# Zero fills copied inside HBM, and one more V window kept on the chip, in a single-token attention layer with its gradients

## The chip, the cores and the metric

The kernel runs on one core of one Trainium2 chip. The metric is the device time of one execution in microseconds (us). Before the change three runs took 816.24, 816.43 and 816.74 us: a median of 816.43 us.

## What is computed

One token passes through a pre-norm attention layer with a cached sliding window and through a bilinear feed-forward layer; the kernel computes the output and the gradients of all inputs for a given output gradient. Cut to what matters:

```
W = 4096                                   # of Sk = 32768 cached positions
k, v = k_cache[:, :, Sk-W:], v_cache[:, :, Sk-W:]        # 8 groups, 256 wide
h  = x + softmax(q k^T / 16) v @ wo,       q = layernorm(x) @ wq
h2 = h + ((n @ w_gate) * (n @ w_up)) @ w_down,   n = layernorm(h)
outputs: h2, and the gradients of x, k_cache, v_cache, wq, wo, w_gate, w_up, w_down
```

The gradients of the two caches (out_2 for K, out_3 for V) are as large as the caches: 8 groups of 32768 x 256 bf16, 16 MB a group. Only the last 4096 positions of a group, 2 MB, carry a gradient. The other 28672 positions, 14336 KB a group, are zero and must be written as zeros: 16 such regions, 234.88 MB together.

## The kernel before

**Two streams.** The zero regions ("fills") are issued by SyncE (`FILL`, hardware queue q1 of the profile), all loads and all other stores by GpSimd (`IO`, software queue q0). Both queues run on the same 16 DMA engines. Each engine's issue order is program order, so a wait of one GpSimd instruction holds all its later DMAs.

**Fills.** Line 58 sets a tile `zeros` of 128 partitions x 8192 bf16 (16 KB a partition) to zero on VectorE. Lines 59 to 62 issue, for each group, a fill of out_2 and one of out_3, whose source is that tile, read 7 times (`NZ`) through a broadcast dimension. 16 fills, each of 896 rows of 16 KB.

**Forward part, by groups g = 0 to 7 (from line 344).** A K or V window is 2 MB, 16 KB a partition, and lies in one of 8 slots of the tile `S`. `K_SLOT` and `V_SLOT` (lines 35, 36) say which: V of groups 0 to 4 have slots 0 to 4 to themselves, K goes around slots 5, 6 and 7, V of 5 and of 6 both use slot 6, and V of 7 takes slot 5. `load_K` and `load_V` call `load_window` (line 79). `scores` transposes K on TensorE and multiplies it with q; `softmax` makes the weights; `moments` (lines 309 to 335) scales K by the weights on VectorE (line 318) and contracts it with V on TensorE (lines 322, 325, 329). V of 5, 6 and 7 share places with other windows, so their loads wait until those are used up: V of 6 waits for the moments of group 5, V of 7 for those of group 6. The halves `woA` and `woB` of the attention's output weight are then loaded over slots 6 and 5 (lines 361 and 376), and the feed-forward weights over slot 7 and the tile `Rt` (lines 377, 378).

**Middle.** Output projection (line 383), feed-forward layer, its gradient and the gradient at the attention output (lines 383 to 460).

**Backward part, by groups (from line 562).** V is transposed again (line 568), the two gradients of a window are made as outer products (line 602), evicted into two of four staging slots 5, 6, 7 and 0 (`STG`) and stored (line 607). V of groups 5, 6 and 7 is no longer on the chip: `V_AGAIN` (line 37) loads it again into slots 1, 2 and 3, once those groups' own V has been used. Gradients of the weights are made in between (`side`, stored at line 477).

Of the kernel before, what the change touches and what calls it, by code (L numbers as in the profile page):

```python
# [7 lines left out]
bf16 = mybir.dt.bfloat16  # L8
# [5 lines left out]
D = 448  # L14
NI = 7
H = 16
G = 8
Dh = 256
W = 4096
T = 32  # L20
F = 1792
FC = 14
Sk = 32768
EPS = 1e-5
SCALE = 1.0 / 16.0
SLOT = T * Dh
NS = 8
NV = 5
HQ = H * Dh // 2
HF = F // 2  # L30
ZW = 8192
NZ = (Sk - W) * Dh // (128 * ZW)


K_SLOT = [5, 6, 7, 5, 6, 7, 5, 7]
V_SLOT = [0, 1, 2, 3, 4, 6, 6, 5]
V_AGAIN = {5: 1, 6: 2, 7: 3}


@with_exitstack  # L40
def kernel(
# [3 lines left out]
    V_, S_, P_ = nc.vector, nc.scalar, nc.tensor  # L45
    FILL = nc.sync
    IO = nc.gpsimd

    const = ctx.enter_context(tc.tile_pool(name="const", bufs=1))
# [4 lines left out]
    FILL.dma_start(out=x_bf[:], in_=A_x.rearrange("a b d -> (a b) d"))  # L54
    go_bf = const.tile([1, D], bf16, tag="rowb", name="go_bf")
    FILL.dma_start(out=go_bf[:], in_=grad_out.rearrange("a b d -> (a b) d"))
    zeros = const.tile([128, ZW], bf16)
    V_.memset(zeros[:], 0.0)
    for g in range(G):
        for o in (out_2, out_3):  # L60
            reg = o[0, g, 0:Sk - W, :].rearrange("s d -> (s d)").rearrange("(p n f) -> p n f", p=128, f=ZW)
            FILL.dma_start(out=reg, in_=zeros[:].unsqueeze(1).to_broadcast([128, NZ, ZW]))


    S = const.tile([128, NS, SLOT], bf16)
    Mt = const.tile([128, G, 2, 2 * Dh], f32)
    Rt = const.tile([128, SLOT], bf16)

    def slot(k):
        return S[:, k, :]  # L70

    def slot_kv(k):
        return S[:, k, :].rearrange("p (t d) -> p t d", d=Dh)

    Kw = [slot_kv(k) for k in K_SLOT]
    Vw = [slot_kv(k) for k in V_SLOT]

    def load_window(dst, cache, g):
        IO.dma_start(out=dst, in_=cache[0, g, Sk - W:, :].rearrange("(p t) d -> p t d", t=T))  # L79

    def load_K(g):
        load_window(Kw[g], A_k_cache, g)

    def load_V(g):
        load_window(Vw[g], A_v_cache, g)
# [174 lines left out]
    def products(Xw, vecT, g, out_ps):  # L260

        for q in range(8):
            tr = ps.tile([128, 4, 2, 128], bf16, tag="tr", bufs=2)
            for i in range(4):
                for dh in range(2):
                    P_.transpose(tr[:, i, dh, :], Xw[:, 4 * q + i, dh * 128:(dh + 1) * 128], ident_bf[:])  # L266
            xt = kt_buf()
            evac(xt, tr[:])
            for i in range(4):
                for dh in range(2):  # L270
                    P_.matmul(out_ps[:, 4 * q + i, :], lhsT=xt[:, i, dh, :], rhs=vecT[:, 4 * g + dh:4 * g + dh + 3:2],
                              start=(dh == 0), stop=(dh == 1))
# [6 lines left out]
    def scores(g):  # L279
        sT[g] = fps.tile([128, T, 2], f32, tag="sT", bufs=2, name="sT")  # L280
        products(Kw[g], qT, g, sT[g])

    def softmax(g):
        s = sT[g]
        pmax = small.tile([128, 2], f32, tag="pmax")
        V_.reduce_max(out=pmax[:], in_=s[:].rearrange("p t h -> p h t"), axis=AX)
        mt = ps.tile([2, 128], f32, tag="tmp", bufs=1)
        P_.transpose(mt[:], pmax[:], ident_f[:])
        gmax = small.tile([2, 1], f32, tag="gmax")
        V_.reduce_max(out=gmax[:], in_=mt[:], axis=AX)  # L290
        gd = small.tile([2, 2], f32, tag="gd")
        V_.tensor_scalar(out=gd[:], in0=ident_f[0:2, 0:2], scalar1=gmax[:, 0:1], scalar2=-SCALE, op0=ALU.mult, op1=ALU.mult)
        nb = ps.tile([128, 2], f32, tag="tmp", bufs=1)
        P_.matmul(nb[:], lhsT=ones_f[0:2, :], rhs=gd[:], start=True, stop=True)
        nbias = small.tile([128, 2], f32, tag="nbias")
        V_.tensor_copy(out=nbias[:], in_=nb[:])
        e = small.tile([128, T, 2], f32, tag="e_f")
        sums = small.tile([128, 2], f32, tag="psums")
        for h in range(2):
            S_.activation(out=e[:, :, h], in_=s[:, :, h], func=ACT.Exp, bias=nbias[:, h:h + 1], scale=SCALE, accum_out=sums[:, h:h + 1])  # L300
        rs = small.tile([128, 2], f32, tag="rsum")
        V_.reciprocal(out=rs[:], in_=total(sums[:], 2)[:])
        pf = small.tile([128, T, 2], f32, tag="p_f")
        V_.tensor_tensor(out=pf[:], in0=e[:], in1=rs[:].unsqueeze(1).to_broadcast([128, T, 2]), op=ALU.mult)
        V_.tensor_copy(out=pT_all[:, g], in_=pf[:])
        p_f[g] = pf

    def moments(g):

        K, Vv, pf = Kw[g], Vw[g], p_f[g]  # L310
        MT = fps.tile([128, 2, 2 * Dh], f32, tag="MT", name="MT")
        acc = fps.tile([128, 8], f32, tag="acc", name="acc")
        for c in range(T // 2):
            pk = pk_buf()
            for i in range(2):
                t = 2 * c + i
                for h in range(2):
                    V_.tensor_scalar(out=pk[:, i, h, :], in0=K[:, t, :], scalar1=pf[:, t, h:h + 1], scalar2=None, op0=ALU.mult)  # L318
            for i in range(2):
                t = 2 * c + i  # L320
                for hf in range(2):
                    P_.matmul(MT[:, hf, :], lhsT=Vv[:, t, hf * 128:(hf + 1) * 128], rhs=pk[:, i, :, :].rearrange("p h d -> p (h d)"),  # L322
                              start=(t == 0), stop=(t == T - 1))
                for hf in range(2):
                    P_.matmul(acc[:, 2 * hf:2 * hf + 2], lhsT=Vv[:, t, hf * 128:(hf + 1) * 128], rhs=pT_all[:, g, t, :],  # L325
                              start=(t == 0 and hf == 0), stop=(t == T - 1), skip_group_check=True)
                for h in range(2):
                    for dk in range(2):
                        P_.matmul(acc[:, 4 + 2 * h + dk:5 + 2 * h + dk], lhsT=pk[:, i, h, dk * 128:(dk + 1) * 128], rhs=ones_bf[:, 0:1],  # L329
                                  start=False, stop=(t == T - 1), skip_group_check=True)  # L330
        S_.copy(out=Mt[:, g, 0, :], in_=MT[:, 0, :])  # L331
        V_.tensor_copy(out=Mt[:, g, 1, :], in_=MT[:, 1, :])
        V_.tensor_copy(out=oT_f[:, 4 * g:4 * g + 4].rearrange("p (h f) -> p f h", f=2), in_=acc[:, 0:4].rearrange("p (f h) -> p f h", h=2))
        V_.tensor_copy(out=kbar[:, 4 * g:4 * g + 4], in_=acc[:, 4:8])
        V_.tensor_copy(out=oT_bf[:, 4 * g:4 * g + 4], in_=oT_f[:, 4 * g:4 * g + 4])

    wo_v = A_wo.rearrange("(b p) n -> p b n", p=128)
    woA = S[:, 6, 0:16 * D].rearrange("p (b n) -> p b n", n=D)
    woB = S[:, 5, 0:16 * D].rearrange("p (b n) -> p b n", n=D)
    wg_sb = S[:, 7, 0:NI * HF]  # L340
    wu_sb = Rt[:, 0:NI * HF]
    bc2 = [S[:, 7, NI * HF:NI * HF + F].rearrange("p (i c) -> p i c", i=2), Rt[:, NI * HF:NI * HF + F].rearrange("p (i c) -> p i c", i=2)]
# [6 lines left out]
    for g in range(G):  # L349
        if g + 1 < NV:  # L350
            load_V(g + 1)
        if g + 2 < 7:
            load_K(g + 2)
        if g == 5:
            load_V(5)
        if g == 6:
            load_V(6)
            load_K(7)
        if g == 7:
            load_V(7)  # L360
            IO.dma_start(out=woA, in_=wo_v[:, 0:16, :])
        softmax(g)
        if g + 1 < G and g != 6:
            scores(g + 1)
        moments(g)
        if g == 6:
            scores(7)
        if g == 0:

            t = ps.tile([128, D], f32, tag="tmp", bufs=1)  # L370
            P_.matmul(t[:], lhsT=ones_bf[0:1, :], rhs=go_bf[:], start=True, stop=True)
            S_.copy(out=dh2_bc[:], in_=t[:])
            for c in range(FC):
                V_.tensor_tensor_reduce(out=wd0[:, c, :], in0=wd0[:, c, :], in1=dh2_bc[:], scale=1.0, scalar=0.0,
                                        op0=ALU.mult, op1=ALU.add, accum_out=d_hh[:, c:c + 1])
# [184 lines left out]
    for g in range(G):  # L560
        if g in V_AGAIN:
            Vw[g] = slot_kv(V_AGAIN[g])
        dp = bps.tile([128, T, 2], f32, tag="dp")
        for q in range(8):
# [6 lines left out]
            for i in range(4):  # L571
                for dh in range(2):
                    P_.matmul(dp[:, 4 * q + i, :], lhsT=xt[:, i, dh, :], rhs=doT[:, 4 * g + dh:4 * g + dh + 3:2],  # L573
                              start=(dh == 0), stop=(dh == 1))
        for again, sl in V_AGAIN.items():
            if sl == g:
                load_window(slot_kv(sl), A_v_cache, again)
# [19 lines left out]
        for c in range(T // 2):  # L597
            d_ps = bps.tile([128, 2, 2, Dh], f32, tag="d2", bufs=2)
            for i in range(2):
                t = 2 * c + i  # L600
# [39 lines left out]
```

## Time and profile before

| what | value |
|---|---|
| median of three runs | 816.43 us |
| profiled execution, time | 816.48 us |
| profiled execution, span | 814.7 us |
| busy: TensorE / VectorE / ScalarE / GpSimd | 504.1 / 374.4 / 165.0 / 40.4 us |
| fills, queue q1 | 234.88 MB, 68.3% of 16 engines' span |
| loads and stores, queue q0 | 103.00 MB, 30.2% of 16 engines' span |
| HBM read / written | 57.28 / 280.59 MB |

The time is 1.8 us longer than the span of the profiled instructions. The span is cut into 40 slices in which a digit is a busy share in tenths. A DMA queue's share is the time that its packets took, over the time of 16 engines. A packet here is one run of bytes that one engine moves; its queue, size, start and duration are recorded. "To landing" is from a DMA's issue to the moment all 16 engines have finished their parts.

### The profile page before, as it was taken

What the parts mean: (1) busy time and instruction counts of PE and PEld (TensorE: products, weight loads), DVE (VectorE), ACT (ScalarE), POOL (GpSimd) and SP (SyncE); (2) the same over time, 40 slices, a digit from 0 to 9 for tenths busy, and PEclk for the clock granted to TensorE, in tenths of its full rate; (3) what the DMA queues carried; (4) which work ended last, traced back from release to release, by engine and by line L of the source; (5) the groups of instructions that cost most, each with busy time, mean ns of one, the idle gap of its engine ahead of it and who ended that gap; (6) DMA issues with size and microseconds to landing.
All of it is one profiled execution on the core that took longest, in us unless ns stands there. A gap on an engine that the chain in (4) does not pass through costs nothing.

```text
span 814.7 us, 12155 instructions
## 1 busy us (share of the span) xinstructions
PE 504.1 (62%) x4991; PEld 301.7 (37%) x4991; DVE 374.4 (46%) x1149; ACT 165.0 (20%) x261; POOL 40.4 (5%) x75
## 2 busy tenths in 40 slices
PE   3559969999566947062995562597597848263200
PEld 3445646666434524031983421243143313010000
DVE  4128837776451644028733470754553626253200
ACT  0230211221101000001012231243343424142100
POOL 3000000000000001000001000001000010000000
PEclk9959878999785969565556555555555555555555
DMA  8999999999999999999999999999999999999993
GB/s 344 430 423 427 430 428 429 425 428 426 430 417 426 415 424 420 428 429 431 426 427 429 409 415 421 431 423 422 404 430 425 425 413 423 421 425 427 424 427 170
DMA packets 24573, 338.66 MB, mean 416 GB/s; under 512 B 1251, under 2 KB 1317, under 8 KB 4677
## 3 DMA queue, kind: packets, MB, share of 16 engines
q1 hardware_dynamic: 14596, 234.88, 68.3%
q0 software_dynamic: 9920, 103.00, 30.2%
q8 instruction: 39, 0.64, 0.3%
q14 instruction: 18, 0.14, 0.0%
HBM read 57.28 MB, written 280.59 MB: 415 GB/s over the span
## 4 chain that ended last, share of the span: by engine, by line
issue 59%; DMA 17%; PE 11%; DVE 4%; POOL 3%; ACT 1%; POOLq 0%; DVEq 0%
DMA S<-in_A_wo_dram 4%; DMA Rt<-in_A_wq_dram 4%; DMA out_dram<-Mt 3%; PE dq_ps L453 3%; DMA S<-in_A_k_cache_dram 3%; DMA S<-in_A_v_cache_dram 2%; PE MT L322 2%; POOL out_dram L477 1%; POOL S L79 1%; DVE Rt L423 1%; POOL out_dram L607 1%; PE dh_ps L159 1%; PE d_ps L602 1%; PE tr L568 1%; PE t L413 1%
## 5 line engine op out<-in xcount | busy, mean ns | idle before, releaser
L602 PE MATMUL d_ps<-R,Mt 32*128 32x512 bf16 x256 | 124.4, 612 | 94.4 <-DVE S L212 93.6
L322 PE MATMUL MT<-Rt,S 128*128 128x512 bf16 x512 | 156.8, 391 | 21.1 <-DMA S<-in_A_v_cache_dram 19.9
L318 DVE TENSOR_SCALAR Rt<-S,pf 128x256 bf16<-128x256 bf16 x512 | 117.8, 283 | 32.0 <-PE acc L329 17.3
L212 DVE CAST S<-d_ps 128x512 bf16<-128x512 f32 x128 | 86.8, 689 | 57.1 <-ACT S L210 43.9
L210 ACT CAST S<-d_ps 128x512 bf16<-128x512 f32 x128 | 75.1, 587 | 171.6 <-PE d_ps L602 171.6
L266 PE MATMUL tr<-ident_bf,S 128*128 128x128 bf16 x512 | 52.5, 267 | 44.5 <-DMA S<-in_A_k_cache_dram 41.2
L602 PEld LDWEIGHTS <-Mt 32*128 32x128 bf16 x256 | 23.2, 113 | 148.1 <-issue 146.7
L325 PEld LDWEIGHTS <-S 128*128 128x128 bf16 x512 | 49.9, 98 | 62.7 <-issue 6.6
L568 PE MATMUL tr<-ident_bf,S 128*128 128x128 bf16 x512 | 68.8, 304 | 3.5 <-ACT Mt L210 3.5
L329 PE MATMUL acc<-ones_bf,Rt 128*128 128x1 bf16 x1024 | 61.8, 163 | 0.0
L568 PEld LDWEIGHTS <-S 128*128 128x128 bf16 x512 | 48.5, 135 | 28.0 <-issue 27.8
L266 PEld LDWEIGHTS <-S 128*128 128x128 bf16 x512 | 41.4, 121 | 42.9 <-DMA S<-in_A_k_cache_dram 41.7
L210 ACT COPY Rt<-tr 128x1024 bf16<-128x1024 bf16 x32 | 32.4, 1012 | 84.7 <-PE tr L266 84.3
L325 PE MATMUL acc<-pT_all,S 128*128 128x2 bf16 x512 | 49.1, 165 | 0.0
L329 PEld LDWEIGHTS <-Rt 128*128 128x128 bf16 x1024 | 44.5, 96 | 0.0
L212 DVE COPY Rt<-tr 128x1024 bf16<-128x1024 bf16 x32 | 22.1, 690 | 48.5 <-PE tr L266 47.0
L210 ACT COPY Mt<-tr 128x1024 bf16<-128x1024 bf16 x32 | 32.4, 1014 | 56.3 <-PE tr L568 29.2
L322 PEld LDWEIGHTS <-S 128*128 128x128 bf16 x512 | 32.0, 97 | 21.7 <-DMA S<-in_A_v_cache_dram 20.4
L331 ACT COPY Mt<-MT 128x512 f32<-128x512 f32 x8 | 4.7, 586 | 164.8 <-PE MT L322 145.4
L573 PEld LDWEIGHTS <-Mt 128*128 128x128 bf16 x512 | 19.9, 108 | 36.7 <-DVE Mt L212 13.7
L573 PE MATMUL dp<-doT,Mt 128*128 128x2 bf16 x512 | 22.6, 168 | 12.3 <-DVE Mt L212 10.5
L212 DVE COPY Mt<-tr 128x1024 bf16<-128x1024 bf16 x32 | 22.0, 686 | 16.4 <-PE tr L568 11.3
(182 smaller groups left out, 435.1 us busy)
## 6 DMA issues: line engine op xcount, KB each, us to landing
out_dram<-zeros SPq DMA_DIRECT2D x16, 14336.0 KB, 149.7
out_dram<-S POOLq DMA_DIRECT2D x16, 2048.0 KB, 29.5
S<-in_A_v_cache_dram POOLq DMA_DIRECT2D x11, 2048.0 KB, 35.6
S<-in_A_k_cache_dram POOLq DMA_DIRECT2D x8, 2048.0 KB, 28.0
out_dram<-Mt POOLq DMA_DIRECT2D x6, 896.0 KB, 22.3
S<-in_A_wq_dram POOLq DMA_DIRECT2D x1, 3584.0 KB, 14.7
S<-in_A_wo_dram POOLq DMA_DIRECT2D x2, 1792.0 KB, 35.4
out_dram<-Mt POOLq DMA_DIRECT2D x3, 1024.0 KB, 35.7
```

The costliest lines, as they stand in the source:

```text
L79: IO.dma_start(out=dst, in_=cache[0, g, Sk - W:, :].rearrange("(p t) d -> p t d", t=T))
L210: S_.copy(out=out, in_=in_)
L212: V_.tensor_copy(out=out, in_=in_)
L266: P_.transpose(tr[:, i, dh, :], Xw[:, 4 * q + i, dh * 128:(dh + 1) * 128], ident_bf[:])
L318: V_.tensor_scalar(out=pk[:, i, h, :], in0=K[:, t, :], scalar1=pf[:, t, h:h + 1], scalar2=None, op0=ALU.mult)
L322: P_.matmul(MT[:, hf, :], lhsT=Vv[:, t, hf * 128:(hf + 1) * 128], rhs=pk[:, i, :, :].rearrange("p h d -> p (h d)"), start=(t == 0), stop=( ...
L325: P_.matmul(acc[:, 2 * hf:2 * hf + 2], lhsT=Vv[:, t, hf * 128:(hf + 1) * 128], rhs=pT_all[:, g, t, :], start=(t == 0 and hf == 0), stop=(t ...
L329: P_.matmul(acc[:, 4 + 2 * h + dk:5 + 2 * h + dk], lhsT=pk[:, i, h, dk * 128:(dk + 1) * 128], rhs=ones_bf[:, 0:1], start=False, stop=(t == ...
L453: P_.matmul(dq_ps[:, 2 * h + dk:2 * h + dk + 1], lhsT=Mt[:, h // 2, hf, c0:c0 + 128], rhs=doT_f[:, 2 * h + hf:2 * h + hf + 1], start=(hf = ...
L568: P_.transpose(tr[:, i, dh, :], Vw[g][:, 4 * q + i, dh * 128:(dh + 1) * 128], ident_bf[:])
L573: P_.matmul(dp[:, 4 * q + i, :], lhsT=xt[:, i, dh, :], rhs=doT[:, 4 * g + dh:4 * g + dh + 3:2], start=(dh == 0), stop=(dh == 1))
L602: P_.matmul(d_ps[:, i, :, :].rearrange("p w d -> p (w d)"), lhsT=rows[32 * k:32 * k + 32, a, :], rhs=R[32 * k:32 * k + 32, :], start=True, ...
```

## The change

The zero tile becomes slot 8 of `S` (now 9 slots), so it is a place for a window like any other. Only the two fills of group 0 read it. The 14 fills of groups 1 to 7 are copies from HBM to HBM: their source is the first run of each partition row of the region of out_2, group 0, which the first fill has written, so they wait for that fill to land. The source run is 8192 elements, read 7 times; for the two fills of group 3 it is 28672 elements (56 KB), read twice. V of group 5 is loaded into slot 8 once both fills of group 0 have landed, and stays. V of 6 takes slot 6 at the place where V of 5 was loaded; V of 7 also goes to slot 6, after the moments of group 6, in two DMAs of 16 positions a partition each. `woA` moves to slot 5 and is issued right behind the second half of V of 7, `woB` to slot 6. In the backward part two windows are loaded again in place of three, into slots 1 and 2.

```diff
-NS = 8
-NV = 5
+NS = 9
+NV = 6
+LONG = 28672
+LONG_G = (3,)
-V_SLOT = [0, 1, 2, 3, 4, 6, 6, 5]
-V_AGAIN = {5: 1, 6: 2, 7: 3}
+V_SLOT = [0, 1, 2, 3, 4, 8, 6, 6]
+V_AGAIN = {6: 1, 7: 2}
...
-    zeros = const.tile([128, ZW], bf16)
-    V_.memset(zeros[:], 0.0)
-    for g in range(G):
-        for o in (out_2, out_3):
-            reg = o[0, g, 0:Sk - W, :].rearrange("s d -> (s d)").rearrange("(p n f) -> p n f", p=128, f=ZW)
-            FILL.dma_start(out=reg, in_=zeros[:].unsqueeze(1).to_broadcast([128, NZ, ZW]))
+    zeros = S[:, 8, 0:ZW]
+    V_.memset(zeros, 0.0)
+    def region(o, g, f):
+        return o[0, g, 0:Sk - W, :].rearrange("s d -> (s d)").rearrange("(p n f) -> p n f", p=128, f=f)
+    for g in range(G):
+        for o in (out_2, out_3):
+            if g == 0:
+                FILL.dma_start(out=region(o, g, ZW), in_=zeros.unsqueeze(1).to_broadcast([128, NZ, ZW]))
+            else:
+                f = LONG if g in LONG_G else ZW
+                n = NZ * ZW // f
+                FILL.dma_start(out=region(o, g, f), in_=region(out_2, 0, f)[:, 0:1, :].to_broadcast([128, n, f]))
...
+    def load_half(dst, cache, g, t0):
+        t1 = t0 + T // 2
+        return IO.dma_start(out=dst[:, t0:t1, :], in_=cache[0, g, Sk - W:, :].rearrange("(p t) d -> p t d", t=T)[:, t0:t1, :])
...
-    woA = S[:, 6, 0:16 * D].rearrange("p (b n) -> p b n", n=D)
-    woB = S[:, 5, 0:16 * D].rearrange("p (b n) -> p b n", n=D)
+    woA = S[:, 5, 0:16 * D].rearrange("p (b n) -> p b n", n=D)
+    woB = S[:, 6, 0:16 * D].rearrange("p (b n) -> p b n", n=D)
...
         if g == 5:
-            load_V(5)
+            load_V(6)
         if g == 6:
-            load_V(6)
             load_K(7)
-        if g == 7:
-            load_V(7)
-            IO.dma_start(out=woA, in_=wo_v[:, 0:16, :])
...
         moments(g)
         if g == 6:
+            for t0 in (0, T // 2):
+                v7 = load_half(slot_kv(V_SLOT[7]), A_v_cache, 7, t0)
+            with tc.issue_after(v7.ins):
+                IO.dma_start(out=woA, in_=wo_v[:, 0:16, :])
             scores(7)
```

## The prediction

> **What bounds the kernel now.** I read the slices first, then the queues, then the landing of the fills, then the stretches of the end. From the page:
>
> ```profile
> span 814.7 us, 12155 instructions
> ...
> DMA  8999999999999999999999999999999999999993
> GB/s 344 430 423 427 430 428 429 425 428 426 430 417 426 415 424 420 428 429 431 426 427 429 409 415 421 431 423 422 404 430 425 425 413 423 421 425 427 424 427 170
> DMA packets 24573, 338.66 MB, mean 416 GB/s; under 512 B 1251, under 2 KB 1317, under 8 KB 4677
> ...
> q1 hardware_dynamic: 14596, 234.88, 68.3%
> q0 software_dynamic: 9920, 103.00, 30.2%
> ...
> HBM read 57.28 MB, written 280.59 MB: 415 GB/s over the span
> ```
>
> The 16 DMA engines are busy from the first slice to the last but one, at 404 to 431 GB/s, while no compute engine is (PE has 62%). The rate is the same whether GpSimd's queue loads (first half) or stores (second half). So the time is bytes over rate plus the two ends, and a wait on a compute engine costs nothing while a fill stands in q1 to use the engines. The stretches of the end (columns: length, then busy time of PE, PEld, DVE, ACT, POOL, then PEclk, DMA share, GB/s):
>
> ```profile
> 440.00:760.00 320.00, 202.91 (x1315) 89.09 (x1313) 153.93 (x285) 108.69 (x167) 20.17 (x33) 0.50 1.01 421
> 760.00:795.00 35.00, 0.22 (x1) 0.00 (x0) 0.70 (x2) 0.59 (x1) 1.06 (x2) 0.50 1.01 427
> 795.00:814.70 19.70, 0.00 (x0) 0.00 (x0) 0.00 (x0) 0.00 (x0) 0.00 (x0) 0.50 0.38 161
> ```
>
> Compute ends at about 762 us; the DMA engines then work off what is queued. After 795 they run out one by one (share 0.38). In the packet records the last store ends at 798.0, most engines finish the last fill at 797 to 805, and the last one at 813.1. So the busiest engine sets the end, and whatever every engine is spared comes off the time. The fills' landings, from the answer on the zero tile:
>
> ```profile
> L62 SPq DMA_DIRECT2D out_dram<-zeros x16: 597/46418/62679, 5.2 to 641.0; - x16
> ...
> DMA to landing us min/median/max: 63.3/149.7/187.2
> ```
>
> The first fill, issued at 5.2, lands at 68.5; the packet records put the end of the second at 135. Packets: of 16 KB, loads and stores alike have a median of 611 ns (91% of the fills' within 625); of 8 KB, 309 ns; the fixed part is then 2 x 309 - 611 = 7 ns, the rest 16384 B in 604 ns = 27.1 GB/s an engine.
>
> **The change, part by part,** against the profiled execution's 816.48 us (span 814.7; 0.05 above the median of 816.43).
>
> 1. *One V window less.* 2 MB are 128 packets of 16 KB, 8 an engine: 8 x 611 = 4.89 us off every engine. No other load or store goes: -4.89.
>
> 2. *Longer packets.* Two fills of 56 rows an engine become 16 rows of 56 KB an engine: 112 packets become 32, 80 x 7 ns = 0.56: -0.56.
>
> 3. *V of 7 in halves.* 16 packets of 309 ns for 8 of 611: +0.06.
>
> 4. *The source of 14 fills.* An engine moves 14 x 56 = 784 packets' worth (16 KB) of copies. Before has no copy inside HBM, so both ends are open. Above: if reading and writing HBM took turns, a packet would cost 2 x 611 ns and the sum 784 x 0.611 = +479 us. A nearer high row is the 39 instruction packets of q8, 16 KB at a median of 942 ns: 784 x 0.331 = +260 us. Below: a copy leaves SBUF out, and if SBUF were what holds the pace, it would be shorter; but 16 KB take 611 ns out of HBM and into it alike, the slope from 8 to 12 to 16 KB is one (309, 460, 611), and no shorter packet of this size is to be found (lowest 608), so I take this for the engine's own pace and exclude a gain. I take the nearest row, 611 ns: **0**, and keep the high ends. What speaks for it: the stretch 40 to 360 us, with many loads beside the fills, runs at 425 GB/s, as the pure writing at the end does. What speaks against it: HBM now is read by the fills too. Read and written were 57.28 + 280.59 = 337.9 MB; 14 x 14.68 = 205.5 MB are added and 2.1 go: 541 MB in 811 us is 667 GB/s on average, where the trace shows no more than 431.
>
> The Trainium skill speaks against this part: "HBM Reference", Specifications, gives a domain about 716 GB/s, so a copy with the engines to itself would get 358 of the 427 it could move. By that figure the stretches in which q0 is quiet grow, and I estimate from it some 36 us more, about 847 instead of 811; no run so far asks for more than 431.
>
> 5. *The copies' wait.* The first copy waits on SyncE for fill 0 (68.5). Behind it stand only the other 13 copies, and nothing else uses that queue. The second zero-tile fill is on the engines from 66.6 to 135, so they have work: 0. Without that cover the engines would idle for an issue and a landing.
>
> 6. *V of 5 into slot 8.* Its load waits for both fills of group 0, 135, and stands in GpSimd's queue between K loads that were issued at 108.05 and 145.52. All later loads are behind it; 10 us of cover, so 0. Should fill 1 land later than 145.5, every later load is late by the difference.
>
> 7. *Loads of the forward part.* The chain of waits had:
>
> ```profile
> 279.34 17.70 DMA S<-in_A_v_cache_dram
> ...
> 315.17 33.41 DMA S<-in_A_wo_dram
> ```
>
> V of 6 is now there a group earlier (its load takes the old place of V of 5 at 197), V of 7 comes in halves as the moments of 6 release them, woA behind it. The chain may be some 18 us ahead at 317 us. Late next is woB, which still waits for the last moments. It gains nothing at the end, since the engines are full: 0. In the backward part two reloads remain where three were (issued at 473, 533 and 562): in step 1 already.
>
> 8. *The long packets beside loads.* Fills 6 and 7 (group 3; counted from 0) ran from 305 to 389, and wo, w_gate and w_up are issued at 280 to 318. If the two queues take turns packet by packet, a small packet of wo (7 KB, 272 ns) waits for 2.1 us (3.5 x 0.604) in place of 0.6. A half of wo has 16 such packets' worth an engine: 16 x 1.5 = 24 us, for both halves and the two feed-forward weights of 8 packets each up to 72, less the 18 of step 7: the chain late by at most 54. The last store is issued at 762 and q1 works until 800: 38 us are covered, and TensorE is busy only 203 of 320 us from 440 on, which takes up the rest. At cost 0; without the cover 16.
>
> Sum: 816.48 - 4.89 - 0.56 + 0.06 = **811.1 us**.
>
> **The rivals.**
>
> A. *Copies cost what fills cost* (forecast): 811.1. Against it only step 4's HBM sum. Its own range is 808.5 to 813.5, for the end of the busiest engine.
>
> B. *HBM holds the copies back where q0 is quiet* (the other side). Where q0 moves a lot, a copy has half the packets and HBM is asked for less; where q0 has nothing, all 427 GB/s are copies and HBM is asked for 854. In the packet records q0 moves under 60 GB/s in eight stretches of 20 us between 160 and 440 us, and q1 has 93% of the bytes there: 148 us. At the price of the 942 ns row they grow by 0.54: +80, 891 us; at the price of 611 nothing. It decides as soon as copies in these stretches take over 3.6% longer (5.4 of 148 us). For it: twice the demand that any slice shows. Against: the flat rate over every mix of reads and writes. Its middle is 811.1 + 40 = 851.
>
> C. *Every copy is slow*: between 811.1 + 260 = 1071 and 811.1 + 479 = 1290. For it speaks only that no row shows a copy.
>
> D. *The gain is lost on the way*: the chain of step 8 outlasts its cover, or the busiest engine is not relieved; 811.1 + up to 16, most likely within 0.2% of before (814.8 to 818.1; about what a measurement of this kernel can tell from no change).
>
> **How the numbers follow.** A 0.55, B 0.33, C 0.06, D 0.06. The likeliest is A: 811.1. Faster by over 0.2%: A, 0.55; within 0.2%: D, 0.06; slower: B and C, 0.39. The range begins at 808, below A's steps, and must reach into B: up to 870 it holds A, D and almost three quarters of B, 0.55 + 0.06 + 0.23 = 0.84; C and B's upper end (0.16) are left out. A alone would be 808.5 to 813.5.
>
> **What would show it.** Right: packets of q1 of 16 KB still near 611 ns and of 56 KB near 2.12 us; slices of 425 GB/s throughout; 336.6 MB in all; HBM read near 261 MB; fill 0 still landing at 68 and no gap in the DMA row after it; V of 5 issued at 135. B: long q1 packets and slices well under 420 GB/s between 160 and 440 us, normal ones after 480; the first copies then take longer than the 42 to 45 us of fills 2 to 5. C: such slices everywhere from 135 on. D: packets of 611 ns, but slices under 8 near the end, with the last stores issued after 800. What would make the forecast wrong is step 4 alone; all other steps together are under 20 us.

## The result, and the profile after

The change makes the kernel slower: 906.38 us (four runs, 904.2 to 907.5) against 816.39 (four runs of before), a ratio of 1.110 [1.108, 1.112]. The profiled execution took 906.39 us. The page after, the lines that answer to those shown of before:

```profile
span 904.6 us, 12152 instructions
...
DMA  8999999999999999999999999999999999999995
GB/s 351 429 426 428 425 430 415 355 363 369 369 356 349 327 380 364 353 324 314 348 343 367 378 396 383 400 395 377 410 381 382 384 393 399 380 407 404 320 317 189
DMA packets 23293, 336.56 MB, mean 372 GB/s; under 512 B 1251, under 2 KB 1317, under 8 KB 4677
...
q1 hardware_dynamic: 13316, 234.88, 70.1%
q0 software_dynamic: 9920, 100.90, 28.6%
...
HBM read 260.70 MB, written 280.59 MB: 598 GB/s over the span
```

The DMA engines are as busy as before and move 2.1 MB less, yet need 90 us more: "busy" now means packets that take longer. The GB/s row tells where. Its first six slices (22.6 us each) are those of before; from the seventh on, where the first copy starts, it lies between 314 and 415 until the tail, and never comes back. HBM read is 203 MB higher. In stretches (length, busy time of PE, PEld, DVE, ACT, POOL, then PEclk, DMA share, GB/s):

```profile
134.00:300.00 166.00, 128.57 (x1816) 83.50 (x1815) 93.46 (x386) 22.24 (x41) 4.87 (x8) 0.85 1.00 367
300.00:440.00 140.00, 60.45 (x502) 44.70 (x500) 52.43 (x181) 6.15 (x10) 3.36 (x4) 0.59 1.00 344
440.00:600.00 160.00, 101.85 (x731) 57.19 (x730) 69.78 (x134) 43.85 (x65) 9.34 (x16) 0.52 1.00 376
600.00:760.00 160.00, 96.27 (x647) 42.45 (x648) 69.94 (x136) 52.68 (x81) 9.72 (x15) 0.50 1.01 390
760.00:842.00 82.00, 26.95 (x59) 6.18 (x58) 22.48 (x37) 16.97 (x29) 2.66 (x5) 0.50 1.01 395
842.00:886.00 44.00, 0.00 (x0) 0.00 (x0) 0.00 (x0) 0.00 (x0) 0.00 (x0) 0.50 1.00 316
886.00:904.60 18.60, 0.00 (x0) 0.00 (x0) 0.00 (x0) 0.00 (x0) 0.00 (x0) 0.50 0.41 160
```

Before had 424, 427, 419 and 423 GB/s in the first four of these. The packet records split the two queues; a copied byte counts twice at HBM (read and written), any other byte once:

| stretch, us | q0, GB/s | copies, GB/s | HBM, read + written |
|---|---|---|---|
| 140 to 300 | 90 | 273 | 636 |
| 300 to 440 | 40 | 303 | 646 |
| 440 to 600 | 112 | 264 | 639 |
| 600 to 760 | 146 | 243 | 633 |
| 760 to 878 | 112 | 258 | 628 |
| 842 to 886 | 0 | 316 | 632 |

What the engines move varies from 316 to 390 GB/s, what HBM delivers hardly at all: 628 to 646. That a copied byte counts twice can be read from the rows themselves: from 600 to 760 us to the last row q0 gives up 146 GB/s, and the copies gain 73, half of it. The 16 KB packets of q1 have a mean of 699 ns (621 before) and a 95th percentile of 1012 (639), while their lowest quarter is still at 611.

### The profile page after: what moved, and what is told of

Its sections match the earlier page's. It is cut to its first block, busy times and chain, and to the rows that moved or that the text cites. A ratio compares the mean times of both kernels' runs of the same rounds, so it can differ in the third digit from the quotient of the medians.

```text
span 904.6 us, 12152 instructions
## 1 busy us (share of the span) xinstructions
PE 506.6 (56%) x4991; PEld 304.1 (34%) x4991; DVE 374.5 (41%) x1149; ACT 164.8 (18%) x261; POOL 40.3 (4%) x75
## 4 chain that ended last, share of the span: by engine, by line
issue 35%; DMA 27%; PE 14%; DVE 5%; another core or an unknown queue 5%; POOL 2%; ACT 1%; POOLq 0%; DVEq 0%
DMA S<-in_A_wo_dram 10%; DMA out_dram<-Mt 8%; DMA S<-in_A_k_cache_dram 5%; DMA Rt<-in_A_wq_dram 4%; PE MT L335 3%; PE dq_ps L466 3%; PE tr L279 1%; POOL out_dram L490 1%; DVE Rt L436 1%; DVE Rt L331 1%; POOL out_dram L620 1%; PE dh_ps L172 1%; PE ao L396 1%; PE acc L342 1%
## 5 line engine op out<-in xcount | busy, mean ns | idle before, releaser
L225 DVE CAST S<-d_ps 128x512 bf16<-128x512 f32 x128 | 87.1, 689 | 58.7 <-ACT S L223 45.2
L396 PE MATMUL ao<-S,oT_bf 128*1 128x448 bf16 x32 | 8.8, 430 | 70.5 <-DMA S<-in_A_wo_dram 70.5
L223 ACT COPY Rt<-tr 128x1024 bf16<-128x1024 bf16 x32 | 32.4, 1012 | 64.8 <-PE tr L279 64.3
L223 ACT COPY Mt<-tr 128x1024 bf16<-128x1024 bf16 x32 | 32.4, 1013 | 62.0 <-PE tr L581 34.9
```

The source lines that it names most:

```text
L223: S_.copy(out=out, in_=in_)
L225: V_.tensor_copy(out=out, in_=in_)
L396: P_.matmul(ao[:], lhsT=oT_bf[:, b:b + 1], rhs=wo_b(b), start=(b == 0), stop=(b == 31))
```

## Experiments

Three theories. **H**: HBM gives some 645 GB/s, read and written together, and copies ask for more ("HBM" stands for the side that all engines share, memory and the way to it; no run here parts the two). **E**: a copy is slow in the engine itself. **S**: re-reading one small source is what is slow. Each experiment is timed against the kernel before in the same session; before was 816.3 to 816.6 in all. The sessions ran on different chips. The edits are shortened.

**The copies by themselves** (phases; one run):

```diff
+    FILL.dma_start(out=blocks(1, 16, 4), in_=blocks(0, 16, 4))   # then 14, 8
+    FILL.dma_start(out=region(1), in_=region(0)[:, 0:1, :].to_broadcast([128, NZ, ZW]))
+    FILL.dma_start(out=big[:], in_=region(1))
+    FILL.dma_start(out=region(1), in_=big[:])
```

> Nothing of the layer is computed; six transfers of the zero region run one after the other, each alone on the engines: a fill from the zero tile, a copy inside HBM over 16, over 14 and over 8 engines (source read once, runs of 16256 B), a copy with one run read 7 times (as in the change), a load of the region, a store of it. Theory H (HBM as a whole gives about 645 GB/s, read and written together): fill, load and store 34 to 35 us each; copies over 16 engines 42 us with packets near 805 ns, over 14 engines 42 us again with packets near 705 ns, over 8 engines 66 us with packets of 606 ns (the engines' own pace); the copy of one run 46 us. Theory E (a copy is slow in the engine itself): packets of about 805 ns in all three, so 42, 48 and 87 us. Theory S (one small source read over and over is what is slow): wide copies at the engines' pace, 32 us over 16 engines, the copy of one run 46 us.

From the packet records: fill 34.4 us, load 34.9, store 34.1, copy over 16 engines 41.2 (mean packet 778 ns), over 8 engines 66.0 (median 606 ns), one run read 7 times 45.2. These are as H had them. S falls: the copies of one run and of the whole region go at the same rate, 325 and 329 GB/s over the transfer. E falls with the 8 engines (66 us, where it had 87). But over 14 engines it was 49.0 us, near E's 48, where H had 42; there the blocks of the engines lay exactly 1 MB apart. So I repeated it with one spacing for all (phases_k; one run):

```diff
+    for k in (16, 14, 12, 10, 8):
+        FILL.dma_start(out=blocks(1, k), in_=blocks(0, k))    # [k, 55 rows], blocks 896 KB apart
```

> Nothing of the layer is computed: the zero region is filled and then copied by 16, 14, 12, 10 and 8 engines one after the other, 55 runs of 16256 B for each engine, the blocks of the engines 896 KB apart in all five (in the earlier phases the blocks of the 14 were 1 MB apart). H (ceiling near 657 GB/s read and written): 16 engines 43.5 us and 14 engines 38 us at 328 GB/s copied; 12 engines just reach it, 33 to 34 us; 10 and 8 engines go at their own pace, packets of 606 ns, 33.4 us. E: the same time, 43 us, with packets near 780 ns, whatever the number of engines.

The whole transfers took 44.1, 41.3, 34.1, 34.3 and 34.1 us, so that of 14 engines was 3 us over H's 38. The main parts of the five copies, ends left out (length, busy time of DVE and POOL, PEclk, DMA share, GB/s copied):

```profile
42.80:83.00 40.20, 0.00 (x0) 0.00 (x0) 1.00 0.99 328
88.90:123.00 34.10, 0.00 (x0) 0.00 (x0) 1.00 0.88 328
132.10:163.00 30.90, 0.00 (x0) 0.00 (x0) 1.00 0.76 317
168.30:199.00 30.70, 0.00 (x0) 0.00 (x0) 1.00 0.63 265
204.50:235.00 30.50, 0.00 (x0) 0.00 (x0) 1.00 0.51 213
```

With 8, 10 and 12 engines the rate goes with the number: 213, 265, 317, at a packet median of 606 ns. From 12 to 14 it gains 11, from 14 to 16 nothing: 328 GB/s copied is 656 read and written. The first microseconds go faster, though. In order: 16 engines from 9 us into their copy on, 14 engines at 2 to 7 us, and 14 engines from 11 us on:

```profile
52.00:80.00 28.00, 0.00 (x0) 0.00 (x0) 1.00 0.99 322
90.90:95.90 5.00, 0.00 (x0) 0.00 (x0) 1.00 0.88 377
100.00:123.00 23.00, 0.00 (x0) 0.00 (x0) 1.00 0.88 321
```

So 14 engines begin at 377, their own pace (754 read and written), and settle at 321, or 642. The ceiling is a rate that holds after some 10 us of copying, and why the start is faster is open. The share of 14 engines, 0.88 of 16, says that they are all occupied; they wait inside their packets (693 ns on average with 14, 790 with 16). H holds for the settled rate; E, which had 43 us and packets near 780 ns for any number, fails with the last three rows.

**The copies in the kernel, all, early and late** (copies_all, copies_early, copies_late):

```diff
-            FILL.dma_start(out=reg, in_=zeros[:].unsqueeze(1).to_broadcast([128, NZ, ZW]))
+            if g >= 1:                      # early: 1 <= g <= 3; late: g >= 4
+                FILL.dma_start(out=reg, in_=reg0[:, 0:1, :].to_broadcast([128, NZ, ZW]))
+            else:
+                FILL.dma_start(out=reg, in_=zeros[:].unsqueeze(1).to_broadcast([128, NZ, ZW]))
```

> Before, with the 14 fills of groups 1 to 7 copied from the first run of the first zero region, all in 16 KB runs; zero tile, slots and loads stay as before. If the copies are the whole cause (H, E and S alike): 906 us as in the change plus 3 to 5 for the V window that is loaded again, 908 to 912. If the changed order of loads or the long runs had the larger part: under 880.

> Before, with only the 6 fills of groups 1 to 3 copied (132 to 389 us of before, where the other queue moves little). H: before's stretches there carry 82 + 2 x 345 = 772 GB/s of HBM traffic against 645, a factor of 1.20 over 257 us: about 866 us. E and S, a fixed price a copy: 6/14 of 95 us: about 857 us.

> Before, with only the 8 fills of groups 4 to 7 copied (389 us to the end, where the other queue moves about 150 GB/s). H: 51 us at a factor of 1.27 and 360 us at 1.068, +39: about 855 us, less than the six early copies cost. E and S, a fixed price a copy: 8/14 of 95 us: about 870 us, more than the six early ones.

All: 897.5 us, 1.099 [1.097, 1.101], so +81.2 comes with the copies alone. (The 908 to 912 expected started from the 906 of another session; the repeats below show sessions 9 us apart.) Early: 852.6, 1.046 [1.043, 1.048], +36.3 or 6.0 a copy. Late: 856.4, 1.049 [1.048, 1.051], +40.0 or 5.0 a copy. The late ones are H's (855) and not the fixed price's (870). The early ones cost less than either had (866, 857), and their total is below that of the late ones, where H had it above: in the order of the two the fixed price was right. With the +81.2 of all 14 in place of 95, a fixed price gives +34.8 and +46.4 for the +36.3 and +40.0 measured, so these two times alone decide little between the theories; phases_k and the rates of the stretches carry more. The six early fills did end 46 us later (434.7 for 388.8), but in that time the other queue went on at its own pace (81 and 62 GB/s in the first two stretches below, 82 and 62 before), which left less for later; my 50 had stretched both. The stretches of the early version, then of the late one:

```profile
134.00:300.00 166.00, 126.94 (x1803) 83.12 (x1802) 93.11 (x384) 22.25 (x41) 4.36 (x7) 0.85 1.00 370
300.00:440.00 140.00, 83.62 (x618) 61.46 (x617) 57.29 (x197) 9.87 (x16) 3.92 (x5) 0.61 1.00 362
440.00:600.00 160.00, 102.72 (x725) 49.19 (x723) 83.57 (x158) 51.51 (x78) 11.33 (x19) 0.51 1.01 424
600.00:760.00 160.00, 101.23 (x603) 41.00 (x603) 71.60 (x131) 56.68 (x89) 9.43 (x15) 0.50 1.01 423
```

```profile
134.00:300.00 166.00, 128.42 (x1794) 84.34 (x1793) 92.57 (x381) 22.26 (x41) 4.36 (x7) 0.83 1.01 425
300.00:440.00 140.00, 82.60 (x634) 60.82 (x632) 58.13 (x201) 9.87 (x16) 3.92 (x5) 0.62 1.01 398
440.00:600.00 160.00, 96.47 (x690) 47.27 (x690) 77.94 (x146) 48.97 (x73) 11.33 (x19) 0.50 1.01 388
600.00:760.00 160.00, 97.76 (x614) 40.61 (x614) 68.79 (x129) 53.36 (x83) 8.90 (x14) 0.50 1.01 398
```

The rate falls where copies are and is back at 424 where they are not. With q0's share counted as above, HBM stands at 653 and 662 in the first two rows of the early version, at 645 and 643 in the last two of the late one.

**Half the copies, in step and out of step** (half_step, half_shift): 98 DMAs of 128 rows, by turns copied and filled; in the second, engines 0 to 7 get 8 packets more at the start.

```diff
+            for n in range(NZ):
+                if n_dma % 2:
+                    FILL.dma_start(out=reg[:, n, :], in_=reg0[:, 0, :])
+                else:
+                    FILL.dma_start(out=reg[:, n, :], in_=zeros[:])
+                n_dma += 1
...
+                    r8 = reg[0:64, 0, :].rearrange("(a b) f -> a b f", b=8)      # half_shift
+                    FILL.dma_start(out=r8[:, 0:7, :], in_=zeros[0:32:4].unsqueeze(1).to_broadcast([8, 7, ZW]))
```

> Before, with the fills of groups 1 to 7 cut into 98 DMAs of 128 rows (8 packets an engine), by turns copied and from the zero tile: half as many copies as in the version with all 14 (897, +81). All 16 engines go through the same turns, so they copy at the same time for the most part. H: about half the price, 816.4 + 40 = 857 us, less as far as the engines drift apart. A fixed price a copy (E, S): 857.

> The same bytes from the same sources as in the version beside it, but engines 0 to 7 get 8 packets of fill more at the start, so that one half of the engines fills from the zero tile while the other half copies. H: HBM is then asked for about 427 + 214 = 641 GB/s at any time, just its ceiling, and the price mostly goes: 819 to 830 us (2.4 of it since engines 0 to 7 end with more work). A fixed price a copy (E, S): 857 plus the same 2.4.

829.7 us, 1.016 [1.014, 1.018], and 833.9, 1.021 [1.019, 1.023]. Half the copies cost 13 us where all cost 81: no fixed price does that; a ceiling that is reached only part of the time can. HBM moved 532 GB/s over the span here (607 with all copies, 415 before). Longer packets are only about 7 of the 13 us: all packets' times, added and divided by 16 engines, are 811.8 us, against 804.8 before and 887.8 with all copies. Most of the rest is an uneven end: in the last 60 us an engine stands idle for 17.9 us on average, 11.8 before. H's own 857 was wrong too, since it took the engines to copy in step. The shift gained nothing, which speaks against that picture and for engines that mix without help; the packet records don't name the engine, so neither is seen directly.

**The source** (wide_source: each copy reads the whole first region once, long runs kept; no_long: the change without 56 KB runs; wide_no_long: both):

```diff
-                FILL.dma_start(out=region(o, g, f), in_=region(out_2, 0, f)[:, 0:1, :].to_broadcast([128, n, f]))
+                src = out_2[0, 0, 0:Sk - W, :].rearrange("s d -> (s d)").rearrange("(n p f) -> p n f", p=128, f=f)
+                FILL.dma_start(out=region(o, g, f), in_=src)
```

> The change, with every copy reading the whole first zero region once (14 MB, in 16 KB or 56 KB runs) in place of one run a partition over and over; as many bytes read and written. H (ceiling on all HBM bytes): 906 us, within 1%. S (the small source is what is slow): near 811 us. A part of it: in between.

> The change, with the two fills of group 3 in 16 KB runs as the others. H: the bytes are the same, so 906 us within 1%; the long packets (2.7 us at the median) were not the cause. If the long runs held the loads of the output weight and so the chain: the first store of a window would be issued some 20 us sooner, but the end stays. If the long packets were themselves slow: under 890 us.

885.1 us, 1.085 [1.083, 1.086], and 897.2, 1.098 [1.096, 1.100]. The first is far from S's 811, but also 2.3% under H's 906. The second should have been 906, so either the long runs cost 9 us or the session differed. Both again beside the change itself:

```diff
-LONG_G = (3,)
+LONG_G = ()
```

> The change itself once more, to stand on the same chip beside the next two. If the 9 us between it (906) and the version without long runs (897) are the long runs' work: 906 again. If they are the difference of two sessions: within 3 us of the version without long runs.

> The change with 16 KB runs only, once more, beside the change on one chip: 897 again, 9 us under the change, if the long runs cost; the same as the change within 3 us if not.

> The change with 16 KB runs only and each copy reading the whole first region once. If reading one small source over and over costs by itself, as 885 against 906 suggested: 12 to 20 us under the version without long runs that stands beside it. If that difference came from elsewhere: equal to it within 3 us. H alone, a ceiling on bytes, predicts equal.

908.3, 1.112 [1.107, 1.116]; 906.1, 1.110 [1.106, 1.114]; 895.2, 1.096 [1.094, 1.098]. In one session the long runs make no difference that the intervals show; the 9 us came with the session or its chip. The wide source is 11 us faster (and 12 in the session before, 885.1 against 897.2), more than H gives (none): re-reading one small source takes a small share of the 90 us. Alone on the engines it had cost nothing (325 against 329 GB/s), and why it does here is open.

**The gain alone** (skip_v5):

```diff
-V_AGAIN = {5: 1, 6: 2, 7: 3}
+V_AGAIN = {6: 2, 7: 3}
```

> Before, without the second load of V of group 5: its part of the backward pass reads the V of group 1 that is still in the slot, so group 5's gradients are left wrong. This prices the gain alone, with no copies. The forecast's step 1: 8 packets of 611 ns less on every engine, 4.9 us less than before, 811.5 us. If the end isn't set by the engines' work: no change, 816.4 us.

811.7 us, 0.9945 [0.993, 0.996]: -4.7, near the 4.9 worked out.

## Why the prediction was wrong

The forecast of 811.1 failed in one step, step 4, "I take the nearest row, 611 ns: 0": the 14 copies cost +81.2 us (copies_all), with 16 KB packets of 699 ns on average in the change. What it gave against itself, 667 GB/s of HBM traffic where no slice showed over 431, was the answer. The row did not bear on the question: every packet of before has one end in HBM, and at 427 GB/s the engines' own pace holds them (phases_k shows a median of 606 ns until 12 engines copy). Every row of before lay below the ceiling, so their agreement over loads and stores said nothing of where it is. "The flat rate over every mix of reads and writes" spoke for the engines, not for HBM.

Rival B had the mechanism but a wrong place: it confined the price to where q0 is quiet, and its highest time was 891. By the signs named ahead, the slow slices came everywhere from 135 us on, as for rival C, but at less than a third of C's price, since its rows (942 ns, 2 x 611) were too high. The ceiling binds in every stretch of the change, since even where before had most on q0 (600 to 760 us: 161 GB/s, fills 262) copies at that pace would ask for 161 + 2 x 262 = 685. The estimate from the Trainium skill's "HBM Reference" (Specifications, 716 GB/s a domain), which worked through all stretches, had the right form and gave 36 us. With the 650 that the runs show, 91% of that figure, the same working gives 82, and copies_all measured +81. The 650 is read from the result and the runs behind it, so this confirms the form of the sum; it is no forecast.

The other steps. 1: right, 4.7 for 4.89; whether it survives in the changed kernel the runs do not tell, for the versions with and without the window were timed in different sessions. 2: nothing to be seen; the 56 KB packets took 2684 ns on average where 2.12 us was expected (the shortest took 2116 ns). A load and a store in phases, which stay below the ceiling, have packets of that size at medians of 2116 and 2121 ns. 5: right, the first copy was issued at 68.66 and no slice is empty. 6: right, V of 5 at 136.5, the next K at 145.8. 7: wrong in place, at no cost. The chain of waits after:

```profile
252.69 41.31 DMA S<-in_A_wo_dram
294.04 0.53 PE ao L396
...
295.18 0.97 PE MT L335 x2
...
314.04 47.76 DMA S<-in_A_wo_dram
361.85 4.96 PE ao L396 x16
```

The earlier woA drew its output projection (`ao`) ahead of the last moments (`MT`) in TensorE's order, so the moments stood 27.6 us behind a DMA (of 70.5 us in which TensorE waited for wo, 28.1 before); woB is issued at 314.04, where it was 315.17. Step 8: the sort of delay was right, its working was not. The packets of 7168 bytes and 272 ns are stores between 440 and 480 us; wo is loaded in packets of 4480 bytes (176 ns), 25 an engine for a half, so 25 x 1.5 = 38 us a half by the same rule in place of 24. In the session that ran both, the first window store was issued at 554 with the long runs and 524 without, the last one at 805 and 772. The end did not move, for the fills went on beyond 900.

## What to carry to other kernels

A copy inside HBM costs HBM twice its bytes. Where a kernel's DMA is at the engines' pace, add up read and written bytes before and after, divide by the time, and if the rate is above anything the trace has shown, treat the row per packet as no evidence: a short run with that one transfer alone, over 8, 12 and 16 engines and well past the fast first 10 us, gives the ceiling. Here the zero tile in SBUF was worth its 16 KB a partition: giving it up cost 81 us, and the window kept in its place was worth 4.7.

## What the runs showed of the hardware

- Copies alone reach 328 GB/s over 16 engines, 656 read and written; in the full kernel the sum is 628 to 662. The engines' own pace (16256 bytes in 606 ns) holds up to 12 copying engines. With 14 engines it also holds for the first microseconds (377 GB/s), before the rate settles at 321.
- Versions that sit at that ceiling differ by 1% between sessions on different chips (the one without long runs 893.5 to 897.4 and 902.1 to 910.9), where before has medians within 0.1%. Compare them within one session.
- The 14-engine copy with blocks 1 MB apart moved 279 GB/s, with 896 KB apart 303, both over the whole transfer. The Trainium skill, "DMA: Bandwidth & Descriptors" (Latency and other measured facts), tells of slower HBM copies at row pitches that are large powers of two. Its pitch is that of partition rows and ours the distance of the engines' blocks, and the two runs differ in rows an engine (60 and 55) too: they point the same way and settle nothing.
